# One K copy of an attention kernel moved from ScalarE to VectorE, ahead of two shifts of q

## The chip, the cores and the metric

One core of a Trainium2 chip. The metric is the device time of one execution in microseconds (us).

The engines are named as in the profile: PE is TensorE's matmuls, PEld its weight loads, DVE is VectorE, ACT is ScalarE, POOL is GpSimd, SP is SyncE (it issues DMAs). L277 is line 277 of the kernel. In the brackets of a profile line stand the idle time in front of it and what ended it; "issue" there means that the profile names nothing that was waited for.

Three words are used throughout. The *lead* is the time by which TensorE's work after the first exponential comes earlier, the *lag* the time by which VectorE's rows come later, and a *gate* is the next thing that TensorE has to wait for.

## The reference, cut to what matters

```python
xn = layernorm(x)                                   # x: 1 x 2048 x 640
q = xn @ wq                                         # 32 heads of 192
p = softmax(einsum("bhqd,bhkd->bhqk", q, k_cache) * 192 ** -0.5)
s = einsum("bhqk,bhkd->bhqd", p, v_cache) ... @ wo
g = silu(swiglu(xn, w1, w3, w2))
return x + s * g
```

The change touches nothing but how K of head 0 gets into its turned (transposed) form in the first 14 us.

## The kernel before: the parts that matter here

The kernel is a stream of steps (head, block of 512 queries, pair of key tiles). A step's scores are computed two steps ahead of its values. Heads from 1 on get turned K by DMA; head 0 gets it from TensorE transposes and copies out of PSUM.

```python
    def copy_k0(copy, src, half, two):               # L277
        KW = loads[0]["KW"]
        ks = slice(half * HP * P, (half + 1) * HP * P)
        copy(out=KW[:, 0:2, ks] if two == 0 else KW[:, 2:5:2, ks], in_=src[:, 2 * two:2 * two + 2, :])
    def shift_k0():                                  # L281
        nc.vector.tensor_copy(out=KW[0:64, 3, :], in_=KW[64:P, 0, :])
    ...
    def project_first():                             # L391 products, L393 qA, L394 qB, L396 qC
        ...
    def shift_first():                               # L400, L401
        nc.vector.tensor_copy(out=qC[64:P, 0, :], in_=qAB[0][0:64, :])
        nc.vector.tensor_copy(out=qC[0:64, 0, :], in_=qAB[0][64:P, :])
    ...
    def head_start():
        ...
        swap_halves(0)                               # xnS: x with its halves swapped, by two DMAs
        copy_k0(nc.scalar.copy, pk0, 0, 0)
        copy_k0(nc.scalar.copy, pk0, 0, 1)
        copy_k0(nc.vector.tensor_copy, pk1, 1, 0)
        load_v(0, (1,))
        load_x(2)                                    # x's third load, 640 KB
        project_first()
        first_scores()
        half_scores()
        turn_k0(pk1, 1, (2, 3))                      # TensorE transposes into pk1
        copy_k0(nc.scalar.copy, pk1, 1, 1)           # <- the copy that moves
        half_scores()
        scores(0)                                    # ends in the first exponential, L513
        shift_first()
        shift_k0()
        scores(1)
        ln_stats(1, 0); ln_stats(1, 1); ln_stats(1, 2)         # L316, L317, L319
        ln_norm(1, 0, nc.vector); ln_norm(1, 1, nc.vector)     # L346
        ln_turn_dma(1, 0); ln_turn_dma(1, 1)                   # DMA transposes of x, L360
        ...
```

A few steps later come head 1's projection (`two_products`, L424, which reads xnT and the swapped xnS; emptied into qA by VectorE, L429, and into qB by ScalarE, L430), then the TensorE transposes of x (`ln_turn(1, 1)`, L354) into the PSUM buffer that those two casts have emptied, then the projection of the second query block (`project0(1)`, L410), which needs the DMA transposes of x.

```python
    def two_products(W, qs):
        ps = ps_st.tile([P, 1024], F32, tag="st2", name="ps")
        for j in range(2 * DC):
            for r in range(2):
                rows = slice(r * 64, (r + 1) * 64)
                xs = xnT if j % 2 == r else xnS
                nc.tensor.matmul(ps[:, r * 512:(r + 1) * 512], lhsT=W[rows, j, :], rhs=xs[rows, j // 2, qs], ...)
```

## Time and profile before

| | before |
|---|---|
| time, median of the first 3 runs | 1938.45 us (1938.1 to 1938.9) |
| span of the profiled run | 1936.2 us (a run of its own, of 1937.93 us, quicker than the three) |
| TensorE busy | 1927.4 us (100%) |
| VectorE, ScalarE busy | 654.3 us (34%), 1179.9 us (61%) |

Busy TensorE says only that its matmuls, which overlap, cover the span (the 16384 value products of L539 last 243 ns each, and together are busy for 849.6 us).

### The profile page before, as it was taken

What the parts mean: (1) busy time and instruction counts of PE and PEld (TensorE: products, weight loads), DVE (VectorE), ACT (ScalarE), POOL (GpSimd) and SP (SyncE); (2) the same over time, 40 slices, a digit from 0 to 9 for tenths busy, and PEclk for the clock granted to TensorE, in tenths of its full rate; (3) what the DMA queues carried; (4) which work ended last, traced back from release to release, by engine and by line L of the source; (5) the groups of instructions that cost most, each with busy time, mean ns of one, the idle gap of its engine ahead of it and who ended that gap; (6) DMA issues with size and microseconds to landing.
All of it is one profiled execution on the core that took longest, in us unless ns stands there. A gap on an engine that the chain in (4) does not pass through costs nothing.

```text
span 1936.2 us, 59673 instructions
## 1 busy us (share of the span) xinstructions
PE 1927.4 (100%) x27275; PEld 1316.6 (68%) x27283; DVE 654.3 (34%) x997; ACT 1179.9 (61%) x1279; POOL 282.5 (15%) x501
## 2 busy tenths in 40 slices
PE   9999999999999999999999999999999999999998
PEld 6666666666666666666666666666666666577776
DVE  7333333333333333333333333333333334521111
ACT  6677677767676767776767776677767677210000
POOL 3111111111111111111111111111111110000000
PEclk9999999999999999999999999999999999999999
DMA  8643433333333434363434343434334220937872
GB/s 181 129 101 68 98 68 88 81 62 83 64 90 61 100 63 97 68 162 69 101 66 100 69 101 69 101 65 101 69 69 97 57 69 2 253 76 136 152 153 60
DMA packets 394643, 178.98 MB, mean 92 GB/s; under 512 B 341616, under 2 KB 382832, under 8 KB 394384
## 3 DMA queue, kind: packets, MB, share of 16 engines
q1 hardware_dynamic: 371136, 125.32, 31.5%
q0 software_dynamic: 19472, 45.71, 10.1%
q8 instruction: 215, 3.52, 0.8%
q10 hardware_dynamic: 3776, 4.06, 0.7%
q14 instruction: 44, 0.36, 0.1%
HBM read 52.82 MB, written 27.79 MB: 42 GB/s over the span
## 4 chain that ended last, share of the span: by engine, by line
PE 99%; DVE 0%; ACT 0%; POOL 0%; issue 0%; POOLq 0%; DVEq 0%; ACTq 0%
PE obank L539 35%; PE st L507 34%; PE ps L424 14%; PE ps_s L111 11%; PE ps_f L754 3%; PE ps_gu L728 1%; PE st L508 1%; PE ps L410 0%; PE pk L592 0%; PE ps L391 0%; PE pst L354 0%; PE pk L271 0%; ACT pT L513 0%; ACT KW L277 0%; POOL W L223 0%
## 5 line engine op out<-in xcount | busy, mean ns | idle before, releaser
L513 ACT ACTIVATE pT<-st 128x1024 bf16<-128x1024 f32 (+1 forms) x1025 | 1046.1, 1021 | 250.1 <-PE st L508 234.0
L539 PEld LDWEIGHTS <-pT 64*128 64x128 bf16 x16384 | 711.2, 94 | 242.7 <-ACT pT L513 0.9
L539 PE MATMUL obank<-vt,pT 64*128 64x193 bf16 x16384 | 849.6, 243 | 0.2 <-ACT pT L513 0.2
L507 PE MATMUL st<-qC,KW 64*128 64x512 bf16 x2046 | 605.7, 376 | 0.0
L548 DVE COPY osum<-obank 128x772 f32<-128x772 f32 x128 | 123.0, 961 | 787.1 <-PE obank L539 787.1
L508 PE MATMUL st<-qB,KW 64*128 64x512 bf16 x1024 | 385.1, 376 | 0.0
L507 PE MATMUL st<-qA,KW 64*128 64x512 bf16 x1022 | 384.4, 376 | 0.1
L508 PE MATMUL st<-qC,KW 64*128 64x512 bf16 x1022 | 384.3, 376 | 0.0
L508 PE MATMUL st<-qA,KW 64*128 64x512 bf16 x1022 | 384.3, 376 | 0.0
L507 PEld LDWEIGHTS <-KW 64*128 64x128 bf16 x3068 | 278.6, 94 | 153.8 <-issue 1.9
L424 PE MATMUL ps<-xnT,W 64*128 64x512 bf16 x1280 | 297.2, 376 | 0.0
L424 PE MATMUL ps<-xnS,W 64*128 64x512 bf16 x1280 | 296.3, 376 | 0.0
L508 PEld LDWEIGHTS <-KW 64*128 64x128 bf16 x3068 | 278.5, 94 | 0.2
L377 POOL DMA_DIRECT2D qC<-qA x124 | 65.4, 528 | 1282.9 <-DVE rl_all L555 1268.2
L430 ACT CAST qB<-ps 128x512 bf16<-128x512 f32 x131 | 76.7, 585 | 228.0 <-PE ps L424 222.4
L111 PE MATMUL ps_s<-wo_sb,oT 128*128 128x384 bf16 (+3 forms) x1535 | 208.8, 299 | 0.1
L424 PEld LDWEIGHTS <-W 64*128 64x128 bf16 x2560 | 122.8, 94 | 121.3
L111 PEld LDWEIGHTS <-oT 128*128 128x128 bf16 x1536 | 148.4, 98 | 60.4
L549 DVE TENSOR_TENSOR osum<-osum,obank 128x772 f32<-128x772 f32 x128 | 122.7, 958 | 13.4
L556 DVE TENSOR_TENSOR ostage<-osum,rl_all 128x768 bf16<-128x768 f32 x128 | 122.6, 958 | 6.0 <-DMA o_scr<-ostage 1.8
L465 DVE SCALAR_TENSOR_TENSOR hT<-pt,qB 64x512 bf16<-64x512 bf16 x64 | 43.8, 684 | 197.7 <-ACT pt L464 197.7
L429 DVE CAST qA<-ps 128x512 bf16<-128x512 f32 x131 | 90.6, 691 | 25.2 <-PE ps L410 7.2
(85 smaller groups left out, 624.0 us busy)
## 6 DMA issues: line engine op xcount, KB each, us to landing
o_scr<-ostage SPq DMA_DIRECT2D x16, 1536.0 KB, 10.5
vt<-in_A_v_cache_dram SPq DMA_DIRECT2D x63, 384.0 KB, 6.0
qC<-qA POOLq DMA_DIRECT2D x248, 64.0 KB, 1.9
qC<-qB POOLq DMA_DIRECT2D x124, 64.0 KB, 2.3
wo_sb<-in_A_wo_dram POOLq DMA_DIRECT2D x1, 7680.0 KB, 37.0
W<-in_A_wq_dram POOLq DMA_DIRECT2D x32, 160.0 KB, 3.6
W<-in_B_w_dram POOLq DMA_DIRECT2D x32, 80.0 KB, 3.3
W<-in_A_wq_dram POOLq DMA_DIRECT2D x32, 80.0 KB, 3.0
```

Source lines behind the costliest of these rows:

```text
L111: nc.tensor.matmul(ps[:, 0:w], lhsT=oT[:, k, :], rhs=wo_sb[:, k, c0:c1], start=(k == 0), stop=(k == OC - 1))
L377: nc.gpsimd.dma_start(out=qC[0:64, half, :], in_=qAB[half][64:P, :])
L424: nc.tensor.matmul(ps[:, r * 512:(r + 1) * 512], lhsT=W[rows, j, :], rhs=xs[rows, j // 2, qs], start=(j == 0), stop=(j == 2 * DC - 1))
L429: a = nc.vector.tensor_copy(out=qAB[0][:], in_=ps[:, 0:512])
L430: b = nc.scalar.copy(out=qAB[1][:], in_=ps[:, 512:1024])
L507: nc.tensor.matmul(st2[:, 0:512], lhsT=ka, rhs=qa, start=r == 0 and nr == 3, stop=r == nr - 1)
L508: nc.tensor.matmul(st2[:, 512:1024], lhsT=kb, rhs=qb2, start=r == 0 and nr == 3, stop=r == nr - 1)
L513: nc.scalar.activation(out=pT2[:, c * w:(c + 1) * w], in_=st2[:, c * w:(c + 1) * w], func=ACT.Exp, scale=att_scale)
L539: nc.tensor.matmul(obanks[r][:, j * 256:j * 256 + DH + 1], lhsT=pT2[r * 64:(r + 1) * 64, t * 512 + j * P:t * 512 + (j + 1) * P], rhs=vt[r ...
L548: nc.vector.tensor_copy(out=osum[:], in_=ov[0])
L549: nc.vector.tensor_tensor(out=osum[:], in0=osum[:], in1=ov[1], op=ALU.add)
L556: nc.vector.tensor_tensor(out=ostage[:, qb * 4:qb * 4 + 4, hg * DH:(hg + 1) * DH], in0=osum[:, :, 0:DH], in1=rl.unsqueeze(2).to_broadcast( ...
```

## The change

Its intent: the copy stands on ScalarE between TensorE's scores and the first exponential. VectorE does such a copy in two thirds of the time (0.68 us against 1.01 us in the trace before), and has the shifts of q and K next, which are not needed at once: in the trace before the last of them ends at 14.34, and the third tile's scores, which read them first, start at 15.68.

```diff
         turn_k0(pk1, 1, (2, 3))
-        copy_k0(nc.scalar.copy, pk1, 1, 1)
+        copy_k0(nc.vector.tensor_copy, pk1, 1, 1)
         half_scores()
```

In VectorE's order it comes after L396 and before L400. Nothing else moves on any engine.

## The prediction

> **What bounds the kernel now.** I read four views, in this order. First the page: TensorE against the span. It is busy 100% of 1936.2 us, which for pipelined matmuls does not yet say that it never waits. So, second, the stretches: the same busy time cut at 14.2, 24.7, 34.7 and 1700 us (columns: stretch, length, then busy time with instruction count of matmul, weight load, VectorE, ScalarE, GpSimd, then clock, DMA share, GB/s).
>
> ```profile
> 0.00:14.20 14.20, 11.23 (x123) 10.02 (x124) 8.59 (x27) 7.69 (x12) 7.24 (x14) 1.00 0.86 232
> 14.20:24.70 10.50, 10.30 (x143) 6.36 (x143) 9.10 (x26) 7.15 (x10) 3.04 (x5) 1.00 1.21 213
> 24.70:34.70 10.00, 9.81 (x119) 5.76 (x122) 8.81 (x23) 5.79 (x8) 1.40 (x2) 1.00 0.75 153
> 34.70:1700.00 1665.30, 1665.04 (x25194) 1130.08 (x25200) 588.53 (x844) 1152.54 (x1238) 263.32 (x466) 1.00 0.40 87
> ```
>
> From 34.7 us on TensorE is covered for 1665.04 of 1665.30 us: there it has no idle time to give, and it will carry to the end whatever lead or lag it has at 34.7 us. The change touches one copy at 13.3 us. So the question is only: by how much does TensorE's work at 34.7 us move? Third, the timeline of 13 to 25 us, where the copy and its neighbours stand (start, duration, engine, line, what; in brackets the idle time before it and what ended it).
>
> ```profile
> 13.07 0.29 DVE L396 COPY qC<-qB 64x512 bf16<-64x512 bf16 x1
> 13.28 1.01 ACT L277 COPY KW<-pk 128x1024 bf16<-128x1024 bf16 x1 [0.29 <-PE pk L271]
> 13.39 0.29 DVE L400 COPY qC<-qA 64x512 bf16<-64x512 bf16 x1
> 13.42 0.39 PE L508 MATMUL st<-qB,KW 64*128 64x512 bf16 x1
> 13.71 0.29 DVE L401 COPY qC<-qA 64x512 bf16<-64x512 bf16 x1
> 13.92 0.42 DVE L281 COPY KW<-KW 64x1024 bf16<-64x1024 bf16 x1
> 14.18 2.01 ACT L513 ACTIVATE pT<-st 128x512 bf16<-128x512 f32 x3
> 14.37 0.89 DVE L316 BATCH_NORM_STATS2 stats<-x_all 128x6 f32<-128x320 bf16 x2
> ...
> 21.32 0.69 DVE L429 CAST qA<-ps 128x512 bf16<-128x512 f32 x1
> ```
>
> The first scores are complete at 13.42 + 0.39 = 13.81 us, but the first exponential starts at 14.18, behind the ScalarE copy. The first value products wait for it, as the fourth view shows: every weight load between 14.3 and 39 us in front of which the weight loader had been idle.
>
> ```profile
> 14.84 0.28 PEld L539 LDWEIGHTS <-pT 64*128 64x128 bf16 x8 [0.47 <-ACT pT L513]
> 15.33 0.28 PEld L539 LDWEIGHTS <-pT 64*128 64x128 bf16 x8 [0.21 <-ACT pT L513]
> 22.52 0.56 PEld L354 LDWEIGHTS <-xn 128*128 128x128 bf16 x10 [0.16 <-issue]
> 24.68 1.85 PEld L410 LDWEIGHTS <-W 128*128 128x128 bf16 x10 [0.23 <-issue]
> 26.95 0.09 PEld L507 LDWEIGHTS <-KW 64*128 64x128 bf16 x1 [0.42 <-issue]
> 34.67 0.09 PEld L507 LDWEIGHTS <-KW 64*128 64x128 bf16 x1 [0.35 <-DVE qA L429]
> 38.72 1.84 PEld L410 LDWEIGHTS <-W 128*128 128x128 bf16 x10 [0.16 <-issue]
> ```
>
> The reader is to see six of them before steady state. The two at 14.84 and 15.33 are the ones the change is aimed at. A change from 64-row to 128-row weights costs 0.16 us (22.52, 38.72, and once more at 53.76); the 0.23 at 24.68 is 0.07 longer. What came then is a DMA: the second transpose of x group 1, issued after 19.4 us and landing 5.1 us later, about 24.6. And at 34.67 TensorE waits for a VectorE cast: a chain that passes ScalarE at 27.88 (exponential), 28.80 (tanh) and VectorE from 29.45 to 34.6.
>
> [...] The trace has both for this very shape, 680 ns (VectorE, once) and 1012 to 1032 ns (ScalarE, three times); I use those. [...] L400[...] starts 0.32 us after the 0.29 us L396, and L281[...] starts 0.21 us after L401, before that has ended. [...] so the copy's full length goes onto the queue.
>
> **The change part by part.** The instruction orders of the two kernels differ in nothing but this: one row leaves ScalarE, one enters VectorE between L396 and L400, and the second accumulator's first product now waits for VectorE (its PSUM bank is the copy's source).
>
> 1. *Removed from ScalarE: 1.01 us.* Only the part on the path counts. ScalarE starts 0.10 us after the last scores' end when idle (24.01 to 24.11, 27.78 to 27.88), so the first exponential can start at 13.81 + 0.10 = 13.91 in place of 14.18: -0.27 us, not -1.01. The values go to 14.57 and 15.06, the third tile's scores from 15.68 to 15.41. V's first half is there (issued 6.36, landing 7.1 later, 13.5).
> 2. *Added to VectorE: 0.68 us.* The source transposes end at 12.63 + 0.61 = 13.24, so the copy runs 13.29 to 13.97, L400 from 14.00 in place of 13.39: +0.61. So too L401 (14.32), L281 (14.53 to 14.95) and group 1's statistics (14.37 to 14.98). Nobody needs the shifts before 15.41 + 0.22, so they are in time, and the copied columns (key tiles 4 to 7) much later.
> 3. *The lead meets a DMA.* Head 1's projection starts at 18.95. With the lead it would be 18.68, but its second operand is the swapped x: issued 11.64, landing 7.2 us later, at 18.84. I allow 18.87. Of 0.27 us some 0.08 stay.
> 4. *The lag meets TensorE.* VectorE has no gap from 13.07 to 19.63, then waits 0.81 us for a GpSimd power which VectorE itself released, so it cannot catch up. L429, the cast that empties the projection's buffer, moves from 21.32 to 21.93 and ends at 22.62 instead of 22.01. The transposes of x (22.52) reuse that buffer: 22.62 + 0.06 (as at 34.67, after a cast ending 34.61) = 22.68. Before, the cast ended 0.5 us before TensorE came; now TensorE comes at 22.44 and waits 0.24. Net +0.16.
> 5. *L410, 24.68.* Without its DMA wait it would have been 24.61; with +0.16 it is 24.77. If the DMA lands as before, net +0.09. I think so, for the transposes of group 1 stand in the queue behind a 640 KB load issued at 13.47 and landing 8.4 us later (21.9), later than either issue even with 0.61 us added.
> 6. *To the end.* The exponential at 27.88 goes to 27.97, and the chain to 34.67 with it: 34.67 becomes 34.76. VectorE has lost its lag there (it waits 0.85 us for the tanh at 29.45), and some 0.1 us that the scores at 28.28 wait for the later shifts of the next query block hide under that chain. From 34.7 us on the +0.09 stays.
>
> Sum: -0.27 at the first exponential, +0.19 at the swapped x, +0.24 at the cast, -0.07 from the DMA wait swallowed: +0.09 us. 1938.45 + 0.09 = 1938.5; I put it at 1938.6, as the errors lie mostly on the late side.
>
> **The rivals.** (a) *The lead survives.* If VectorE's lag were smaller, say the cast was done by 22.38, step 4 costs nothing. Even then L410 waits for its DMA at 24.6: 24.68 stays 24.68, and the end is where it was, 1938.4. Only if that DMA came earlier too could up to 0.08 us be won. Against: VectorE's rows leave no gap to absorb 0.6 us. (b) *The DMA moves with VectorE.* The transposes at 18.06 are issued when VectorE has normalised x; the issue goes 0.61 us later. If landing follows issue, not the queue, it comes at 25.2, L410 at 25.29, and 0.6 us are lost to the end: 1939.05. For it: little DMA traffic is seen at 22.5 to 23.5. I give it one in four. (c) *The new copy is slower or waits more*, 0.75 us added: then step 4 is +0.3 and the end 1938.7. (d) *TensorE is the bound and hides all*: true after 34.7 us only, where it carries the lag, and so can hide none.
>
> **Range and chances.** Three runs before spread over 0.8 us (1938.1 to 1938.9), as much as any effect here. Rivals a to c give 1938.4 to 1939.05; with 0.4 us of spread below and above I take 1938.0 to 1939.3. Two per cent are 39 us. No chain above holds even 1 us, so within 2% is as good as certain[...].
>
> **What would show it right or wrong.** In the new profile: first exponential at 13.9 (step 1); the new VectorE copy at 13.3, 0.68 us, and L316 at about 14.98 (2); L424's first product at about 18.9, not 18.7 (3); an idle wait of the weight loader in front of L354, about 22.68, named as VectorE's cast or x (4); L410 at 24.7 to 24.8 (5), at 25.2 if rival b holds; the wait at 34.67 at 34.7 to 34.8 (6). The prediction is wrong if L354 starts before 22.5, if L410 starts after 25, or if the lag at 34.7 us is not that at the end.

What is cut above, at the marks, said how long copies take and when an instruction of VectorE has to wait for those before it, without a trace or run that shows it, and set chances aside for a slow run. No term of the sum is cut: it came to -0.27 + 0.19 + 0.24 - 0.07 = +0.09 us. "This very shape" is the copy of 1024 bf16 columns out of PSUM. Step 2's +0.61 us rests on two figures of the trace before: such a copy took 0.68 us, and L400 started at 13.39, 0.03 us after the end of L396 (13.07 + 0.29). That L400 would wait for the new copy's end in the same way, and the copy not for that of L396, was the author's estimate. The "little DMA traffic" of rival (b) is 5 GB/s from 22.5 to 23.5, against 178 GB/s in the 1 us before. That the load ahead of the x transposes in their queue decides when they land (step 5) was an estimate, too; no run shows it.

## The result, and the profile after

| | before | after |
|---|---|---|
| time, median of 6 runs each | 1938.35 us (1938.05 to 1938.9) | 1938.26 us (1938.03 to 1938.75) |
| ratio | | 1.0, 95% interval 0.9987 to 1.0013 |
| span of the profiled run | 1936.2 us (time 1937.93 us) | 1936.5 us (time 1938.32 us) |
| first exponential starts | 14.18 us | 14.05 us |
| VectorE, ScalarE busy | 654.3, 1179.9 us | 655.0, 1180.3 us |

No difference in time is seen: 0.09 us between medians of runs that spread over 0.8 us, and the interval allows 2.5 us either way. A lead of 0.3 us that reached the end would be hard to see in such times, too; that it gets lost is read from the traces.

The two profiles cannot be laid over each other by absolute time. In the run after, everything up to the second cast of q (L393, 12.61 us before, 12.80 after) was 0.19 us later on all engines, ahead of anything that the change touches. From here on I count from the start of that cast (a copy that changes the type), called t0, and write +1.57 for 1.57 us after it. VectorE and ScalarE in the changed kernel (timeline):

```profile
13.47 0.69 DVE L277 COPY KW<-pk 128x1024 bf16<-128x1024 bf16 x1
14.19 0.28 DVE L400 COPY qC<-qA 64x512 bf16<-64x512 bf16 x1
14.05 2.00 ACT L513 ACTIVATE pT<-st 128x512 bf16<-128x512 f32 x3 [0.87 <-PE st L508]
15.17 0.89 DVE L316 BATCH_NORM_STATS2 stats<-x_all 128x6 f32<-128x320 bf16 x2
21.97 0.69 DVE L429 CAST qA<-ps 128x512 bf16<-128x512 f32 x1
```

The copy and its two neighbours are where the prediction had them: the copy takes 0.69 us, the statistics come 0.61 us later (+2.37 in place of +1.76), the exponential 0.32 us earlier (+1.25 in place of +1.57). ScalarE now sits idle 0.87 us and waits for the scores. The weight loads in front of which TensorE's loader had been idle:

```profile
15.18 0.28 PEld L539 LDWEIGHTS <-pT 64*128 64x128 bf16 x8 [0.20 <-ACT pT L513]
19.15 1.82 PEld L424 LDWEIGHTS <-W 64*128 64x128 bf16 x18 [0.33 <-issue]
22.71 0.56 PEld L354 LDWEIGHTS <-xn 128*128 128x128 bf16 x10 [0.16 <-DVE qA L429]
25.05 1.85 PEld L410 LDWEIGHTS <-W 128*128 128x128 bf16 x10 [0.42 <-issue]
27.33 0.09 PEld L507 LDWEIGHTS <-KW 64*128 64x128 bf16 x1 [0.42 <-issue]
35.05 0.09 PEld L507 LDWEIGHTS <-KW 64*128 64x128 bf16 x1 [0.36 <-DVE qA L429]
39.09 1.85 PEld L410 LDWEIGHTS <-W 128*128 128x128 bf16 x10 [0.16 <-issue]
```

Read against the lines of before: a new wait of 0.33 us stands at 19.15, inside head 1's projection. The loads at 22.71 and 25.05 are at +9.91 and +12.25 (before: +9.91 and +12.07). So the lead of 0.32 us is gone by the projection, and TensorE is 0.18 us behind at L410. What the two waits are for, as TensorE's timeline and the chain of work that ended last show in the same kernel (start, length, what):

```profile
18.81 0.38 PE L424 MATMUL ps<-xnT,W 64*128 64x512 bf16 x1
19.15 0.39 PE L424 MATMUL ps<-xnS,W 64*128 64x512 bf16 x2
```

```profile
13.55 0.62 DVE KW L277
...
20.30 4.65 DMA xnT<-xn
24.95 0.14 issue
25.08 2.32 PE ps L410 x10
```

The first product of the projection, on x itself, comes with the lead (+6.01, before +6.34). The first on the swapped x waits until 19.15, that is +6.35, as before: the DMA of the second half was issued at 11.83 and took 7.3 us, to about 19.1. At L410 it is the DMA transpose of x, landing at 24.95. The chain that ended last has changed its way: before, it passed ScalarE's copy (13.28) and then TensorE; now it passes the moved copy and VectorE's rows to the issue of that transpose at 20.30. In the changed kernel's first profile VectorE is thus on the path, but by way of a DMA and not of the cast.

### The profile page after: what moved, and what is told of

The parts are those of the page before. It is cut to its first block, busy times and chain, and to the rows that moved or that the text cites. A ratio compares the mean times of both kernels' runs of the same rounds, so it can differ in the third digit from the quotient of the medians. Undisturbed runs are those within 1.5% of the kernel's fastest.

```text
span 1936.5 us, 59680 instructions
## 1 busy us (share of the span) xinstructions
PE 1928.2 (100%) x27283; PEld 1316.9 (68%) x27283; DVE 655.0 (34%) x998; ACT 1180.3 (61%) x1278; POOL 282.5 (15%) x501
## 4 chain that ended last, share of the span: by engine, by line
PE 98%; DVE 1%; DMA 0%; ACT 0%; issue 0%; DVEq 0%; ACTq 0%
PE obank L539 35%; PE st L507 33%; PE ps L424 14%; PE ps_s L111 11%; PE ps_f L754 3%; PE ps_gu L728 1%; PE st L508 1%; PE ps L410 0%; DVE stats L316 0%; DMA xnT<-xn 0%; DMA x_all<-in_A_x_dram 0%; PE ps L391 0%; DVE xn L346 0%; DVE mv L317 0%; PE pst L354 0%; PE pk L271 0%
## 5 line engine op out<-in xcount | busy, mean ns | idle before, releaser
L548 DVE COPY osum<-obank 128x772 f32<-128x772 f32 x128 | 123.1, 962 | 787.0 <-PE obank L539 787.0
L430 ACT CAST qB<-ps 128x512 bf16<-128x512 f32 x131 | 76.8, 586 | 228.4 <-PE ps L424 222.9
L111 PE MATMUL ps_s<-wo_sb,oT 128*128 128x256 bf16 (+3 forms) x1536 | 208.8, 299 | 0.0
```

The lines of the kernel that those rows point to most:

```text
L111: nc.tensor.matmul(ps[:, 0:w], lhsT=oT[:, k, :], rhs=wo_sb[:, k, c0:c1], start=(k == 0), stop=(k == OC - 1))
L430: b = nc.scalar.copy(out=qAB[1][:], in_=ps[:, 512:1024])
L548: nc.vector.tensor_copy(out=osum[:], in_=ov[0])
```

## The experiments

Every profile is one execution, so the table counts from that run's t0. "Swapped x" is the first product of head 1's projection that reads it, "x transposes" the first weight load of L354, "L410" its first weight load, "later cast" the weight load that waits for the cast of head 1's second query block. "L410 of block 2" is an absolute time far enough in that nothing of the head follows. e5 and e6 are not in the table; their numbers stand with them.

| run | t0 | exponential | swapped x | x transposes | L410 | later cast | L410 of block 2 | span |
|---|---|---|---|---|---|---|---|---|
| before | 12.61 | +1.57 | +6.35 | +9.91 | +12.07 | +22.06 | 38.72 | 1936.2 |
| after | 12.80 | +1.25 | +6.35 | +9.91 | +12.25 | +22.25 | 39.09 | 1936.5 |
| e8 (after, again) | 12.68 | +1.24 | +7.69 | +11.25 | +13.47 | +23.47 | 40.20 | 1937.6 |
| e1 (no copy) | 13.10 | +1.24 | +6.00 | +9.56 | +11.83 | +21.82 | 38.98 | 1936.4 |
| e2 (no copy, no DMA waits) | 12.89 | +1.24 | none | +9.57 | +11.66 | +21.63 | 38.57 | 1936.0 |
| e3 (after, no DMA waits) | 12.65 | +1.25 | none | +9.90 | +11.98 | no wait | 40.07 | 1937.4 |
| e11 (e3 again) | 12.67 | +1.24 | none | +9.89 | +11.98 | no wait | 38.68 | 1936.0 |
| e7 (before, no DMA waits) | 12.84 | +1.57 | none | +9.90 | +11.99 | +21.97 | 38.86 | 1936.5 |
| e4 (after, more lag) | 12.65 | +1.25 | +6.71 | +10.81 | +12.90 | +23.16 | 39.86 | 1937.5 |
| e9 (copy shared) | 12.79 | +1.25 | +6.01 | +9.62 | +11.71 | +21.69 | 38.53 | 1935.9 |
| e10 (shared, no DMA waits) | 12.96 | +1.25 | none | +9.63 | +11.71 | +21.69 | 38.70 | 1936.1 |

One reading holds for all rows, and for e5 and e6: the span less the time of "L410 of block 2" is 1897.3 to 1897.7 us in every profile (1897.48 before, 1897.41 after, 1897.33 in e3, 1897.64 in e4). Whatever the first 38 us gain or lose is carried to the end, and the spread between the profiled runs arises there too. On times alone no run can be told from the kernel before: the 95% interval of every ratio includes 1. Where times are compared below, it is by medians and ranges of five runs, and is no more than that.

The edits of e1, e2, e3, e7, e10 and e11 make part of the computation wrong. The comparison with the reference is too coarse to see these errors.

**e1: the copy made by nobody.** Its columns are zeroed at 1.1 us, when VectorE waits for x. This gives ScalarE's part of the change without VectorE's.

```diff
         load_k0(0, nc.sync)
+        nc.vector.memset(loads[0]["KW"][:, 2:5:2, HP * P:2 * HP * P], 0.0)
...
-        copy_k0(nc.scalar.copy, pk1, 1, 1)
```

> The copy is made by nobody (its columns are set to zero early, while VectorE waits for x; the result is wrong on purpose): ScalarE is free as after the change, VectorE is free as before it. Times counted from the start of the second qA cast (before: 12.61 us, after: 12.80 us); before / after the change were: first exponential +1.57 / +1.25, first product with swapped x +6.35 / +6.35, weight load of the x transposes +9.91 / +9.91, first weight load of the next query block's projection (L410) +12.07 / +12.25, weight load after the wait for the cast +22.06 / +22.25. Theory (the lead of the first exponential ends at the swap's DMA, and only VectorE's lag moves what comes later): +1.25, +6.35, +9.91, +12.07, +22.06; time as before within 0.3 us. Rival (the lead is eaten by VectorE's copy): without it the lead of 0.3 us stays to the end, +22.06 becomes about +21.75, time 0.3 us below before.

Measured: 1938.39 us against 1938.45 before (5 and 9 runs), ratio 1.0001. The profile is that of the rival, though the 0.3 us that it had promised in time are not seen: the lead passes the swapped x (+6.00), is still 0.35 us at the x transposes, and 0.24 us at L410 and after. My expectation that the swap's DMA always takes the lead was wrong: in this run t0 was 0.49 us later than before while the swap landed 6.9 us after its issue, in time. Whether this gate closes differs from run to run. So the swap alone cannot be what takes the lead in general; VectorE's lag, which is missing here, has to be tested by itself.

**e7: the kernel before, with TensorE's two DMA waits taken away** by reading other data that is there already. This is the control.

```diff
-    def two_products(W, qs):
+    def two_products(W, qs, swapped=True):
...
-                xs = xnT if j % 2 == r else xnS
+                xs = xnT if j % 2 == r or not swapped else xnS
...
-        cast_pair(qAB, two_products(loads[h]["W"], slice(qb * 512, (qb + 1) * 512)))
+        cast_pair(qAB, two_products(loads[h]["W"], slice(qb * 512, (qb + 1) * 512), (h, qb) != (1, 0)))
...
     def project0(qb):
...
-        qs = slice(qb * 512, (qb + 1) * 512)
+        qs = slice(0, 512) if qb == 1 else slice(qb * 512, (qb + 1) * 512)
```

> The kernel before with the two DMA waits taken away: the control. Theory: it has no lead to lose, so only the 0.07 us at L410 go: +1.57, +6.35, +9.91, +12.00, +21.99; time as before or 0.1 us less. If it gains 0.3 us or more, the DMA waits cost the kernel before more than its trace shows, and the theory of the lead is not needed.

The profile moves as expected: +11.99 at L410 and +21.97 later, 0.08 and 0.09 us earlier than before; nothing else. The time is 1938.04 us against 1938.45, more than I had allowed, though the ranges overlap (1937.91 to 1938.57, and 1937.94 to 1938.78). By my own rule this says two things. The DMA waits may cost the kernel before more in some runs than its one profile shows; e8 shows such a run, of the changed kernel. And the times do not need the theory of the lead, since the control gains without one. So the lead and its loss are shown by the traces alone; what the DMA waits cost on average is not settled by five runs.

**e2: no copy and no DMA waits** (the edits of e1 and e7 together).

> As the run without the copy, and TensorE's two waits for DMAs are taken away by other data (head 1's first projection reads x itself in place of the swapped x; the projection of query block 1 reads group 0; wrong on purpose). Theory: with neither DMA in its way the lead of 0.3 us survives: first product of head 1's second operand at about +6.03, transposes +9.6, L410 +11.7, the weight load after the cast +21.7; time 0.3 to 0.4 us below before. Rival (something else than the two DMAs absorbs it, e.g. VectorE's cast or the next x load): +22.0 and the time of before.

With both gates open the lead goes through to the end. Weight loads in e2:

```profile
15.27 0.28 PEld L539 LDWEIGHTS <-pT 64*128 64x128 bf16 x8 [0.21 <-ACT pT L513]
22.46 0.56 PEld L354 LDWEIGHTS <-xn 128*128 128x128 bf16 x10 [0.16 <-issue]
24.55 1.84 PEld L410 LDWEIGHTS <-W 128*128 128x128 bf16 x10 [0.16 <-issue]
...
30.97 1.82 PEld L424 LDWEIGHTS <-W 64*128 64x128 bf16 x18 [0.19 <-issue]
...
34.52 0.09 PEld L507 LDWEIGHTS <-KW 64*128 64x128 bf16 x1 [0.16 <-DVE qA L429]
```

From the first values to L410 the loader idles only the 0.16 us that stand in front of this change of weight height (0.16 to 0.18 us in the 13 profiles, where nothing else was waited for; the 0.42 us of the change back, at 26.81, are left out above). Of the two later waits, that at 30.97 comes when the next swap of x lands (about 30.9), and that at 34.52 is the one for the later cast, shorter here than before (0.16 us in place of 0.35), so the first costs nothing in the end. +9.57, +11.66 and +21.63 are 0.34, 0.41 and 0.43 us earlier than before, and 0.33, 0.33 and 0.34 us earlier than e7, the control with the same waits removed: nothing else absorbs the lead. Time: 1937.77 us, the lowest median (1937.59 to 1938.12), ratio 0.9997. That is 0.27 us below e7, about the lead, but the two ranges overlap.

**e3 and e11: the changed kernel without the DMA waits** (the edits of e7 alone, on the changed kernel). This isolates VectorE's lag.

> The changed kernel with the two DMA waits taken away in the same manner. Theory: the lead reaches the projection (+6.03) but then TensorE waits for VectorE's lagging cast, transposes at about +9.91 as in the changed kernel; L410 follows at +12.0 without its DMA, the load after the cast at +22.0: 0.25 us earlier than the changed kernel, about 0.07 earlier than before. Rival (VectorE's lag costs TensorE nothing, the DMAs all): +9.6 and +21.7, as in the run with no copy.

> The changed kernel with no DMA waits once more: the first such profile fell on a run in which x's third load came 1 us late. Theory: transposes +9.91, held by VectorE's cast, L410 +11.98, load after the cast +21.97; the two long runs of the first time (1939.0 and 1939.3) come back only where that load is late.

Both profiles show the wait that the theory asked for. In e11:

```profile
22.56 0.56 PEld L354 LDWEIGHTS <-xn 128*128 128x128 bf16 x10 [0.49 <-DVE qA L429]
24.65 1.84 PEld L410 LDWEIGHTS <-W 128*128 128x128 bf16 x10 [0.16 <-issue]
```

TensorE comes 0.33 us early, then stands until VectorE's cast has emptied the buffer: 0.49 us of idle loader, 0.16 of them the change of height. The transposes start at +9.89, where they started before the change. VectorE alone takes the whole lead, with no DMA in sight. e5 and e6 below, which read all the right data, agree (e5 is the changed kernel itself up to this place): there the swapped x came in time (+6.01), and the loader stood 0.49 and 0.51 us for the same cast. In e5:

```profile
22.75 0.56 PEld L354 LDWEIGHTS <-xn 128*128 128x128 bf16 x10 [0.49 <-DVE qA L429]
```

Times: 1937.97 us (e3) and 1938.13 us (e11), against 1938.45 and 1938.52 before; none of e11's five runs was long (at most 1938.42).

The profile of e3 fell on its longest run (1939.27 us), and shows what made that one long. VectorE, and TensorE's loader:

```profile
23.62 0.89 DVE L316 BATCH_NORM_STATS2 stats<-x_all 128x6 f32<-128x320 bf16 x2 [1.12 <-DMA x_all<-in_A_x_dram]
```

```profile
25.49 1.82 PEld L410 LDWEIGHTS <-W 128*128 128x128 bf16 x9 [0.76 <-issue]
```

x's third load landed 10.0 us after its issue (8.4 us before, 7.3 in the profile after). VectorE's statistics waited for it, the copy of the x transposes behind them came late, and TensorE waited 0.76 us, until just after that copy (it ended at 25.43, the wait at 25.49). The profile names no cause; as the products of this run read other columns of x, I infer that they waited for the PSUM buffer which the copy empties.

**e8: the changed kernel once more**, unchanged, for a second profile.

> The changed kernel once more, for a second profile and more times. Theory: the first exponential at +1.25, the cast at +9.15 and the transposes not before +9.88 whatever the DMAs do, for they are held by the cast; L410 between +11.98 (no DMA wait) and +12.3; the time 1938.0 to 1938.8, not to be told from before.

Four runs took 1937.92 to 1938.13 us; the fifth, the profiled one, 1939.38. Its TensorE:

```profile
20.37 0.39 PE L424 MATMUL ps<-xnS,W 64*128 64x512 bf16 x2 [0.95 <-DMA xnS<-xnT]
```

Here the swap landed 8.6 us after its issue, at 20.3, and everything after it is 1.3 us later. The cast waited 0.80 us for TensorE and came at +10.05, not at +9.15; so the cast did not hold the transposes, as I had expected whatever the DMAs did, and VectorE's lag and the lead are both hidden. My upper limit of +12.3 for L410 was too low for such a run. In the two long profiles, e3 and e8, several DMAs were late together: the swap took 9.2 and 8.6 us and x's third load 10.0 and 9.7 us, where the other profiles have at most 7.6 and 8.4 us. Over the 13 profiles this one DMA, 320 KB from SBUF to SBUF, took 6.7 to 9.2 us.

**e4: VectorE's lag made larger**, by doing an idempotent shift three times.

```diff
         shift_first()
-        shift_k0()
+        shift_k0(); shift_k0(); shift_k0()
```

> The changed kernel with VectorE's lag made larger: the shift of head 0's K (0.42 us) is done three times in place of once (the result stays right), after the copy and before the statistics. Times counted from the start of the second qA cast; the changed kernel had: statistics +2.37, cast of head 1's q +9.17, weight load of the x transposes +9.91, L410 +12.25, load after the later cast +22.25. Theory (the cast is where TensorE meets VectorE's lag, and there is no slack left in the changed kernel): statistics +3.3, cast +10.1, transposes +10.8, L410 +12.9, +22.9; the time 0.6 to 0.8 us above the changed kernel. Rival (VectorE's lag is hidden, the DMAs alone set TensorE): +9.91 stays, and the time too.

```profile
23.46 0.56 PEld L354 LDWEIGHTS <-xn 128*128 128x128 bf16 x10 [0.71 <-DVE qA L429]
25.55 1.84 PEld L410 LDWEIGHTS <-W 128*128 128x128 bf16 x10 [0.16 <-issue]
```

+0.91 us of lag at the cast (+10.08 in place of +9.17) became +0.90 us at the transposes (+10.81). The test is not clean, for the third tile's scores read the shifted K: in this run TensorE waited 0.56 us for the shift itself at 15.96, before it came to the projection. Even so it stood 0.55 us at the cast beyond the change of height. L410 came at +12.90 as expected. By the later cast (+23.16) 0.26 us more were lost than I had expected: two score products of the next query block (29.49 and 29.81) each came 0.32 us after the one before, where in the changed kernel a pair follows every 0.21 us, while VectorE did the shifts that they read, late now; the values came late with them, and VectorE's sum of the values (L548), without a wait in the changed kernel, waited 0.18 us for TensorE. Time 1939.23 us against 1938.08 for the unlengthened kernel of the same rounds, every run above 1939.0; the expectation had been 0.6 to 0.8 us. The cast is where TensorE meets VectorE, and no slack is left there.

**e5: VectorE's order altered** so that x's late third load could not hold the copy L356.

```diff
         if qb == 0 and p == 3:
-            ln_stats(2, 0)
             ln_turn(1, 1, nc.vector.tensor_copy)
+            ln_stats(2, 0)
```

> The changed kernel with VectorE's order altered at one place: the copy of x group 1's transposes (L356) ahead of group 2's first statistics, which wait for x's third load. In the profile of the run with no DMA waits that load landed late, the statistics waited 1.1 us for it, the copy behind them came 1.0 us late and TensorE waited 0.76 us at L410. Theory: this is what makes single runs of these kernels 1 us longer; with the order altered L410 has no gap of that kind, no run is above 1938.9, and the median is that of the changed kernel or up to 0.2 us less. Rival (the long runs come from elsewhere): the spread of 0.8 to 1.5 us stays.

A miss: 1939.2 us, all five runs within 1938.96 to 1939.47, about 1 us slower than the changed kernel. First VectorE, then TensorE's loader:

```profile
23.52 0.82 DVE L356 COPY xnT<-pst 128x1280 bf16<-128x1280 bf16 x1 [0.83 <-PE pst L354]
```

```profile
28.95 0.09 PEld L507 LDWEIGHTS <-KW 64*128 64x128 bf16 x1 [0.59 <-DVE qA L429]
```

VectorE now idles 0.83 us for TensorE's transposes, in which it did the statistics before. So it is late with the next cast (+15.36 in place of +14.64), and TensorE waits 0.59 us there. L410 itself had no gap (+11.98), as foreseen; the cost moved one station on. The trace has 0.52 us of it at L410 of block 2 (39.66, which is +26.81; +26.29 in the changed kernel).

**e6: the same, with x's third load issued by GpSimd**, so that it no longer stands ahead of the DMA transposes in SyncE's queue.

```diff
         load_v(0, (1,))
-        load_x(2)
...
         ln_stats(1, 1)
+        load_x(2, queue=nc.gpsimd)
```

> As the run with the order altered, and x's third load is issued by GpSimd after group 1's first reciprocal root, so that the transposes of group 1 do not stand behind it in SyncE's queue. Theory (the transposes' landing, not their issue, is set by that queue): their landing is earlier, L410 follows TensorE's own work at +11.98, and the load after the cast is at +21.97, 0.28 us before the changed kernel; the time 0.1 to 0.3 us below it. Rival (landing follows the issue 4.6 to 5.8 us later whatever stands in the queue): L410 stays at +12.25. Risk: the third load now lands too late for its statistics, and the end moves out by up to 1 us.

A miss too: 1939.17 us. The loader waited 1.18 us for the transposes:

```profile
26.05 1.85 PEld L410 LDWEIGHTS <-W 128*128 128x128 bf16 x10 [1.18 <-DMA xnT<-xn]
```

L410 came at +13.03, 0.78 us later than in the changed kernel. The two transposes landed 6.4 and 5.4 us after issue, while the load moved out of their queue was in flight beside them from 18.5 to 23.3. In this one profile, being in another queue did not help them. As e6 carries e5's reordering, and that costs 1 us by itself, its time says nothing about the queue; and the landing is one sample, within what the same transposes did in SyncE's queue (+12.93; +11.78 to +13.78 in five other profiles).

**e9: the copy shared**, half on ScalarE in the idle time which the change has left there, half on VectorE. The fourth group of transposes goes to the bank of the first, so that the two engines read two PSUM banks; what they would do in one bank, no run here shows.

```diff
-        turn_k0(pk1, 1, (2, 3))
-        copy_k0(nc.scalar.copy, pk1, 1, 1)
+        KW0, k1 = loads[0]["KW"], slice(HP * P, 2 * HP * P)
+        for a, d in ((2, 2), (3, 0)):
+            for b in range(HP):
+                nc.tensor.transpose(out=pk1[:, d, b * P:(b + 1) * P],
+                                    in_=k0["v"][:, HP + b, FIRST[a]:FIRST[a] + P], identity=ident_bf[:])
+        i0 = nc.scalar.copy(out=KW0[:, 2, k1], in_=pk1[:, 2, :])
+        i1 = nc.vector.tensor_copy(out=KW0[:, 4, k1], in_=pk1[:, 0, :])
+        tc.declare_no_dep(i1.ins, i0.ins, reason="two banks, two destinations")
```

> The copy is shared: 512 columns by ScalarE in the 0.87 us in which it sits idle before the first exponential, 512 by VectorE, from two PSUM banks (the fourth group of transposes goes to the bank of the first; the result stays right). Times counted from the start of the second qA cast. Estimate from the trace's own casts of 512 columns: ScalarE 0.6 us, over before the scores are there; VectorE 0.4 us in place of 0.69. Theory: first exponential still at +1.25 to +1.3, VectorE's statistics at +2.07 in place of +2.37, its cast at +8.86 in place of +9.17, so the transposes of x are held to +9.6 in place of +9.91 where the DMAs allow it. Time at best 0.3 us below the changed kernel, and hidden whenever the swap's DMA is late. Rival (a split copy delays the first exponential or nothing is gained): exponential at +1.5, transposes +9.9.

Casts of 512 columns on ScalarE took 0.58 to 0.59 us (L430, before and after). On VectorE the traces had no copy of 512 bf16 columns yet; the 0.4 us are an estimate, near the 0.42 us of 256 f32 columns (L393, before), and in this run the copy took 0.42 us.

The two halves in the timeline, and TensorE's loader behind them:

```profile
13.45 0.59 ACT L635 COPY KW<-pk 128x512 bf16<-128x512 bf16 x1 [0.29 <-PE pk L633]
13.46 0.42 DVE L636 COPY KW<-pk 128x512 bf16<-128x512 bf16 x1
```

```profile
22.41 0.56 PEld L354 LDWEIGHTS <-xn 128*128 128x128 bf16 x10 [0.21 <-DVE qA L429]
24.50 1.84 PEld L410 LDWEIGHTS <-W 128*128 128x128 bf16 x10 [0.16 <-issue]
```

The exponential stays at +1.25, the cast is at +8.89, the x transposes at +9.62: of a lead of 0.34 us at the projection (+6.01) 0.29 us are kept, 0.05 us go to the cast. The span, 1935.9 us, is the shortest of all profiles, but the profile fell on the quickest of the five runs (1937.78 us). The time, 1938.24 us against 1938.52 before (5 and 9 runs, ratio 0.9999, interval 0.9985 to 1.0012), is not to be told from either kernel.

**e10: the copy shared, and no DMA waits** (wrong).

> The shared copy with TensorE's two DMA waits taken away by other data (wrong on purpose). Theory: transposes at +9.6, L410 +11.7, load after the later cast +21.7, as in the run with no copy and no DMA waits: VectorE is no gate any more; time 0.3 us below the changed kernel with no DMA waits of the same chip. Rival (any work added to VectorE there is paid): +9.75 and +21.85 or later.

+9.63, +11.71 and +21.69, as expected, within 0.06 us of e2, in which nobody made the copy. In time, 1938.01 us against 1938.13 for e11 of the same rounds, it does not stand out, and the expected 0.3 us are not confirmed by the times, only by the trace.

## Why the prediction was right, point by point

The time lay in the range (1938.26 us; 1938.0 to 1939.3), and the class "within 2%" held. That tests little: all six runs of the kernel before lie in that range as well. The mechanism, an early exponential whose lead is lost to a DMA and to VectorE's lag, held too, in the traces. Not every term of the sum had its size, and one of the signs that I had named for being wrong came up: L410 started at 25.05, after 25. Of that, 0.19 us stand in front of anything that the change touches; counted from t0 it corresponds to 24.86 in the run before. The sign was too sharp for runs whose t0 lies up to 0.49 us apart. The wait in front of L354 was named as VectorE's cast, as foreseen, but it is no longer than the change of height, 0.16 us.

1. *First exponential, -0.27.* Measured -0.32. ScalarE answered 0.05 us faster than the 0.10 us I had taken from later places.
2. *VectorE, +0.61.* Measured +0.61 at the statistics. The order of the instructions and the two figures of the trace before gave it to 0.01 us: the copy starts 0.21 us after the start of the 0.29 us L396, before that has ended, and L400 starts 0.03 us after the copy's end, as it had after that of L396 before.
3. *The lead meets the swapped x, +0.19, 0.08 left.* Measured: nothing left in the profile after. This term hangs on the DMA, which lands in time in e1, e5, e6 and e9 and far too late in e8. I had treated one landing, 7.2 us, as a constant; it was 6.7 to 9.2 us.
4. *The cast, net +0.16.* Mis-sized; measured 0.00. I let the cast follow VectorE's lag of 0.61 us in full. But before the change the cast did not wait for VectorE. Its two predecessors in the kernel before:

```profile
20.44 0.80 DVE L346 TENSOR_SCALAR xn<-x_all,mv,rstd 128x640 bf16<-128x640 bf16 x2 [0.81 <-POOL rstd L327]
20.90 0.38 PE L424 MATMUL ps<-xnT,W 64*128 64x512 bf16 x1
```

   The last product ends at 21.28, and the cast starts at 21.32. In the changed kernel, where VectorE sets it, the cast starts 0.72 us after the L346 pair; by that it could have started at 21.16 before. So about 0.15 us of the lag fell into that gap, and the cast came 0.46 us late (+9.17 in place of +8.71). With that, cast and TensorE arrive together. e2, e11, e5 and e6 show that the cast is nevertheless the gate which I took it for: it closes at +9.90 with the copy on VectorE and is not felt at +9.57 without it.
5. *L410, net +0.09.* Measured +0.18, by another way: L410 waited for the DMA transpose, which I had held fixed and which landed 0.18 us later, its issue being 0.62 us later (+7.50). Whether the issue did that is not shown. With the issue at +7.50 it landed at +11.78 to +13.78 in five profiles (e5, e11, after, e8, e3), with the issue at +6.9 at +11.73 to +11.98 in four (e1, e2, before, e7): two of the late issues landed as early as the early ones, so a landing does not simply follow its issue, as rival (b) had it. (b)'s 0.6 us were not seen in the profile after. What sets the landing stays open.
6. *To the end.* Measured: +0.18 at L410, +0.19 at the later cast, and the span follows "L410 of block 2" within 0.4 us in every run. In the changed kernel TensorE is covered for 1665.17 of 1665.30 us from 34.7 us on, as before:

```profile
34.70:1700.00 1665.30, 1665.17 (x25202) 1129.70 (x25197) 589.20 (x845) 1153.94 (x1237) 263.29 (x466) 1.00 0.40 87
```

So the trace counted +0.19 us where I had said +0.09, and the medians -0.09 us, which is noise. Errors of steps 3, 4 and 5 partly cancelled, which is luck. What is shown: each of the two gates is enough to take the lead (e11, e5 and e6 for VectorE, the profile after and e8 for the swap), and with both open, and L410's transposes not waited for, it reaches L410 of block 2, from where every span runs on alike (e2). What is not shown: the mean effect of the change on the time, for which the six runs of each kernel give 0.09 us and the interval up to 2.5 us either way; how often each gate closes in runs that were not profiled; why the DMAs' landings scatter; and what set t0 apart by up to 0.49 us.

## What to carry to other kernels

Work taken off one engine's path is worth only the distance to the next gate: look at once for the next thing that the freed engine will wait for, here a buffer which the newly loaded engine empties 8.5 us later. When you shift a lag along an engine, ask at each station what that station waited for before; slack in front of it eats the lag, and only the rest is felt. Where transfers scatter by more than the effect, argue from distances inside one trace and repeat the profile: one landing is a sample, not a constant.

## Further figures that the traces give

- Copies of bf16 out of PSUM: VectorE took 680 to 692 ns for 1024 columns (before and after) and 0.42 us for 512 (e9, e10); ScalarE 1012 to 1032 ns for 1024 (before and after) and 0.59 us for 512 (e9, e10).
- A change of the weights' height: the loader's idle time in front of the first weights of the other height was 0.16 us (0.17 us in e1 and e8, 0.18 us in e5) on the way from 64 to 128 rows, behind products of 193 columns, where no other wait stood. On the way back it differed with the products in front: 0.10 to 0.11 us behind transposes of 128 columns and 0.42 to 0.43 us behind products of 512, in all 13 profiles; 0.21 us behind products of 256 (before, after and e9).
- The landing of one and the same DMA, 320 KB between SBUF partitions, each time issued about 0.97 us before t0, took 6.7 to 9.2 us over 13 profiles.
